# Attention and feed-forward on one core: the first batch in one pass, a later first feed-forward chunk, and another way to split float64 weights

## The chip, the cores and the metric

One Trainium2 chip, of which the program uses one core. The metric is the device time of one execution in microseconds. The engines are named as in the profile: PE (TensorE, with PEld for its weight loads), DVE (VectorE), ACT (ScalarE), POOL (GpSimd) and SP (SyncE, which issues all the transfers here).

## The reference: what is computed

Attention over 8 batches of 8 heads (576 rows, head width 64) in which, row by row, only the scores within tau of the row's maximum count; then a feed-forward with softplus on its 4608 tokens.

```python
scores = scale * np.matmul(q, k.transpose(0, 1, 3, 2))
thresh = np.max(scores, axis=-1, keepdims=True) - tau
scores = np.where(scores >= thresh, scores, -1000000000.0)
attn = np.exp(scores - np.max(scores, axis=-1, keepdims=True))
attn = attn / (np.sum(attn, axis=-1, keepdims=True) + 1e-09)
x = (attn @ v), heads side by side            # [4608, 512] float32
h = x @ w_in                                  # w_in [512, 2048], float64
g = np.maximum(h, 0.0) + np.log1p(np.exp(-np.abs(h)))
out = (g @ w_out).astype(np.float32)          # w_out [2048, 512], float64
```

The two weight matrices arrive as float64, everything else as float32.

## The kernel before

**Numbers.** Every matrix product is done on float32r words, a high and a low one: `hi_of` rounds to the high word, `lo_of` subtracts it, and products of three parts (high by high, high by low, low by high) are added in PSUM. So each weight element, too, has to become a high and a low word.

**Attention.** A *unit* is a batch and a pair of heads; a *tile* is 128 query rows of a unit. A unit has nine tiles; there are 32 pairs of batch and heads, so 288 tiles. For each unit, POOL splits k, q and v (`split_k`, `split_q`, `split_v`), PE transposes them and ACT copies them out. For each tile PE makes the scores (`scores`), DVE takes the row maximum (`row_max`, L397), ACT the exponential (`exps`, L405), DVE masks and sums (`mask`, L410), PE transposes the weights (`weights_T`, L441), ACT and DVE split them (`weights_hi`, `weights_lo`, L462 and L124), and PE multiplies by v (`values`).

**Feed-forward.** A *chunk* of tokens goes through `hidden` (PE, 16 blocks of w_in), `softplus` (ACT), `parts_of` (DVE and POOL) and `project` (PE, w_out), whose sums are collected by `project_out`. One matmul of 512 columns is a unit of work here; a chunk of 512 tokens has 384 of them (192 in `hidden`, 192 in `project`), one of 256 tokens half as much. `stream` is one long generator of these matmuls, and the main loop draws some of them at each attention tile. `target(g)` says how many shall be done by tile g: chunk n runs evenly from tile `first[n]` to `first[n + 1]`, the last two and what is left after the attention at their own pace.

**The first batch in two passes.** With `NSPLIT = 1` the first batch goes through each pair of heads twice: units of kind "one" (tiles 0, 1, 5, 6, so the first 256 rows of both heads) for four pairs, then units of kind "two" (the other five tiles) for the same four pairs. Each pass loads, splits and transposes k, and loads and splits v, again. The first two chunks then have 256 tokens, and the first of them can begin as soon as the four units "one" are done:

```python
first.append((b * 9 + (4 if b < NSPLIT and o < 256 else 9)) * NPAIR + (LAG0 if b < NSPLIT else LAG))
```

With `LAG0 = LAG = 8` that is tile 24 for the first chunk, 44 for the second, and 80, 116, 152 and so on for those of 512 tokens.

**Weights.** `to_f32` makes the words of one piece (128 rows of 512 weights); there are 32 pieces, taken from the list `WL` one every `W1` tiles. A piece is loaded (512 KB), then worked on in `first` two tiles later and in `second` one tile later. Its words of w_in are stored to `wi_d` in DRAM (two transfers of 256 KB), from which each chunk loads its blocks again (512 KB each, 16 per chunk); those of w_out stay in SBUF. Six DVE operations, two of ACT (three for w_out) and one of POOL make a piece.

**Order.** All engines take their instructions in order, and a scheduler sets each engine's order when the program is built. PSUM has two score banks (`banks`) and four others (`ps_g`). Where `row_max` and `weights_T` compare with `TG`, an early tile has its threshold made by ACT (L399) and its transposes put into `ps_g`; a later one has the threshold made by DVE (L401) and the transposes put into its own score bank.

Of the kernel before, what the change touches and what calls it, by code (L numbers as in the profile page):

```python
# [10 lines left out]
F32R = mybir.dt.float32r  # L11
U32 = mybir.dt.uint32
AF = mybir.ActivationFunctionType
ALU = mybir.AluOpType
# [7 lines left out]
W_MIN = 2.0  # L22
W_MAX = (122880.0 - 2.0 ** -7) * 2.0 ** 16
# [16 lines left out]
WS = 3  # L40
LT = 4
WB = 3
NSPLIT = 1
LAG = 8
NMM = 10.3
HD = (1, 1)
# [1 line left out]
PAIR = 2  # L48
NST = 4
GV = 1  # L50
TG = 45
W1 = 1.1
W0 = 1
SPA = 0

# [2 lines left out]
def tile_kernel(ctx: ExitStack, tc: tile.TileContext, q, k, v, tau, w_in, w_out, out):  # L58
# [8 lines left out]
    nc = tc.nc  # L67
# [7 lines left out]
    NPAIR = H // 2  # L75
# [30 lines left out]
                            op0=ALU.is_ge, op1=ALU.mult)  # L106
# [8 lines left out]
    def hi_of(eng, out_, in_):  # L115
        if eng is nc.gpsimd:
            eng.tensor_scalar(out=out_, in0=in_, scalar1=1.0, scalar2=1.0, op0=ALU.mult, op1=ALU.mult)
        elif eng is nc.scalar:
            eng.copy(out_, in_)
        else:  # L120
            eng.tensor_copy(out_, in_)  # L121

    def lo_of(eng, out_, in_, hi):
        eng.tensor_tensor(out=out_, in0=in_, in1=hi.bitcast(F32), op=ALU.subtract)  # L124
# [8 lines left out]
    def to_f32(src, want, name, then):  # L133

        keep = 1 if want else 0
        while free[0] < 3 + keep and free[0] < NFC - held[0]:
            force()
        if free[0] >= 3 + keep:
            took = 3
            fm = piece(F32, f"wa_{name}")  # L140
            f, m = fm[:, 0, :], fm[:, 1, :]
            s = piece(F32, f"wb_{name}")[:, 0, :]
            st = piece(U32, f"wc_{name}").rearrange("p a n -> p (a n)")
        else:
            took = 0
            st = fpool.tile([P, 2, DM], U32, tag="acc", name=f"wc_{name}").rearrange("p a n -> p (a n)")
            f, m, s = [fpool.tile([P, 512], F32, tag="st", bufs=NST, name=f"w{t}_{name}") for t in ("sw", "se", "st")]
        free[0] -= took + keep
        held[0] += keep
        w = piece(F32R, f"wo_{name}") if want else None  # L150

        def done():
            free[0] += took

        if src.dtype == F32:
            nc.sync.dma_start(f, src)

            def parts(h, l):
                hi_of(nc.scalar, h.bitcast(F32R), f)
                lo_of(nc.gpsimd, l, f, h.bitcast(F32R))  # L160
            defer(WD, lambda: then(parts, w, m, s, done))
            return
        nc.sync.dma_start(st, src.bitcast(U32))
        words = st.rearrange("p (n t) -> p n t", t=2)
        low, high = words[:, :, 0], words[:, :, 1]
        fu, mu, su = f.bitcast(U32), m.bitcast(U32), s.bitcast(U32)

        def first():  # L170
            nc.scalar.activation(m, high.bitcast(F32), AF.Abs, scale=2.0 ** 16)
            nc.vector.tensor_scalar(out=fu, in0=high, scalar1=23, scalar2=None, op0=ALU.logical_shift_left)
            nc.vector.scalar_tensor_tensor(out=fu, in0=low, scalar=9, in1=fu,
                                           op0=ALU.logical_shift_right, op1=ALU.bitwise_or)
            nc.scalar.activation(f, fu, AF.Copy, scale=2.0 ** -43)
            nc.vector.tensor_scalar(out=m, in0=m, scalar1=W_MIN, scalar2=W_MAX, op0=ALU.max, op1=ALU.min)
            nc.vector.tensor_scalar(out=mu, in0=mu, scalar1=3, scalar2=0xFFFFF000,
                                    op0=ALU.logical_shift_left, op1=ALU.bitwise_and)
            defer(1, second)

        def second():
            nc.vector.scalar_tensor_tensor(out=su, in0=high, scalar=0x80000000, in1=mu,
                                           op0=ALU.bitwise_and, op1=ALU.bitwise_or)
            nc.vector.tensor_scalar(out=mu, in0=su, scalar1=0xFF800000, scalar2=None, op0=ALU.bitwise_and)

            def parts(h, l):
                if w is not None:
                    hi_of(nc.scalar, h, s)
                nc.gpsimd.tensor_tensor(out=l, in0=f, in1=m, op=ALU.mult)
            then(parts, w, s, f, done)  # L190

        defer(WD, first)

    ready = set()
# [58 lines left out]
    for b in range(B):  # L253
        for kind in (("one", "two") if b < NSPLIT else ("all",)):
            for hp in range(NPAIR):
                s = Unit()
# [137 lines left out]
    def row_max(s, t):  # L394
        negm = apool.tile([P, 1], F32, tag="negm", bufs=3, name=f"negm_{s.i}_{t}")
        thr = apool.tile([P, 1], F32, tag="thr", bufs=3, name=f"thr_{s.i}_{t}")
        nc.vector.reduce_max(negm, s.sp[t][:, :, 0:HS], axis=AX.XY, negate=True)  # L397
        if 9 * NPAIR * s.b + t < TG:
            nc.scalar.activation(thr, negm, AF.Identity, bias=ntau, scale=-1.0)  # L399
        else:  # L400
            nc.vector.tensor_scalar(out=thr, in0=negm, scalar1=-1.0, scalar2=ntau, op0=ALU.mult, op1=ALU.add)  # L401
        s.m[t] = (negm, thr)
# [24 lines left out]
    def weights_T(s, t):  # L427
        half = s.half[t]
        e = e_all[:, half, :]
        other, second = mate(s, t)  # L430
        lone = other is None
        if s.b * 9 * NPAIR + t < TG:
            main = ps_g.tile([P, NC, P], F32, tag="g", name=f"tm_{s.i}_{t}")
            rest = ps_g.tile([P, NC, P], F32, tag="g", name=f"tr_{s.i}_{t}")[:, 0, :] if lone or second else None
        else:
            sp = s.sp[t]
            main = sp[:, 0, :].rearrange("p (c n) -> p c n", n=P)
            rest = sp[:, 1, 0:P]
        for c in range(NC):
            c0 = half * SR + c * P  # L440
            nc.tensor.transpose(main[:, c, :], e[:, c0:c0 + P], ident)  # L441
        if lone:
            r0 = 0 if half else SM
            nc.tensor.transpose(rest[0:SR, :], e[:, r0:r0 + SR], ident)
        elif second:
            nc.tensor.transpose(rest, e_all.rearrange("p h n -> p (h n)")[:, SM:SM + P], ident)  # L446
        s.sp[t] = (main, rest)
# [85 lines left out]
    def load_x(u, cc):  # L533
# [3 lines left out]
        while c < u.T:  # L537
            b, o = divmod(u.t0 + c, S)
            m = min(S - o, u.T - c)
            for kind in (("all",) if b >= NSPLIT else ("one", "two")[o >= 256:1 + (o + m > 256)]):  # L540
                need("x", b, cc, kind)
# [176 lines left out]
    def defer(n, f):  # L718
        if n == 0:
            f()  # L720
        else:
            later.append((now["p"] + n, f))
# [11 lines left out]

    tiles = [(s, t) for s in units for t in s.tiles]
    NS = len(tiles)
    WL = [("i", 0), ("i", 1), ("o", 0), ("i", 2), ("i", 3), ("o", 1), ("o", 2), ("o", 3)]

    chunks, first = [], []
    while sum(u.T for u in chunks) < NT:  # L740
# [4 lines left out]
        b, o = divmod(u.t0 + u.T - 1, S)  # L745
# [107 lines left out]
    done = 0.0  # L853
    for g, (cur, t) in enumerate(tiles):
# [5 lines left out]
        for step in PAT:  # L860
# [20 lines left out]
            elif step == "w":  # L881
                while prep and prep[0][0] <= g:
                    _, f, a = prep.pop(0)
# [41 lines left out]
```

## Time and profile before

| | us |
|---|---|
| three runs | 1540.53, 1544.3, 1549.28; median 1544.3 |
| the profiled execution | 1545.64 |
| its span, first to last instruction | 1543.5 |
| busy in the span: PE, DVE, ACT, POOL | 1410.7, 1073.9, 917.8, 588.1 |
| exponentials (L405), one per tile | first at 18.8, last at 1335.1 |

The exponential of a tile is the clock of this document: "tile 44 at 271.8" means that the 45th instruction of L405 began 271.8 us after the first instruction. Stretches between such times show what a tile costs in each part of the program. A busy PE is not PE at its peak: its matmuls overlap, and their ends are modelled. Durations of neighbouring instructions overlap a little as well, so sums of durations exceed busy times.

### The profile page before, as it was taken

How to read it: one execution, taken by the hardware profiler on the slowest of the kernel's cores; microseconds unless marked ns; L12 is line 12 of the kernel's file. 1: busy time of each engine (PE TensorE's matmuls, PEld its weight loads, DVE VectorE, ACT ScalarE, POOL GpSimd, SP SyncE). 2: the span in 40 equal slices, each digit the busy share in tenths (PEclk: the TensorE clock that was granted, in tenths of full speed). 3: DMA queues.
4: the chain of work that ended last, by engine and by line, in shares of the span. 5: the costliest groups of instructions: out<-in, count | busy, mean ns of one | idle time of the engine just before them, and what ended most of it. 6: DMA issues, size and time to landing. Idle time of an engine off the chain costs nothing.

```text
span 1543.5 us, 24467 instructions
## 1 busy us (share of the span) xinstructions
PE 1410.7 (91%) x8076; PEld 1202.7 (78%) x8076; DVE 1073.9 (70%) x2372; ACT 917.8 (59%) x1861; POOL 588.1 (38%) x612
## 2 busy tenths in 40 slices
PE   4555778889899999999999999999999999999998
PEld 4444767778788888888888888888888888878887
DVE  7999798778777777777777777777777777511212
ACT  5565676677576657666776576666666666511110
POOL 4554445334243334334433433344334332242321
PEclk9776899999999999999999999999999999999999
DMA  6767764544343355434443353335334532352331
GB/s 171 217 184 207 244 204 133 172 132 127 106 126 113 108 130 144 116 112 118 149 115 104 100 160 102 108 110 147 111 106 114 146 105 77 101 173 96 118 101 41
DMA packets 142030, 202.44 MB, mean 131 GB/s; under 512 B 38192, under 2 KB 97872, under 8 KB 141904
## 3 DMA queue, kind: packets, MB, share of 16 engines
q1 hardware_dynamic: 141904, 200.89, 44.6%
q8 instruction: 64, 1.05, 0.3%
q14 instruction: 62, 0.51, 0.1%
HBM read 152.44 MB, written 27.41 MB: 117 GB/s over the span
## 4 chain that ended last, share of the span: by engine, by line
PE 61%; ACT 10%; DVE 8%; issue 4%; DMA 3%; POOL 2%; SPq 1%; POOLq 0%; ACTq 0%; DVEq 0%
PE s L391 8%; PE o L636 6%; PE o L632 6%; PE o L634 6%; PE h L574 6%; PE s L441 6%; PE h L576 6%; PE h L578 6%; PE pv L485 3%; PE pv L486 3%; ACT L596 2%; DVE e_all L410 2%; ACT gH L462 2%; ACT st L596 2%; ACT L405 1%
## 5 line engine op out<-in xcount | busy, mean ns | idle before, releaser
L124 POOL TENSOR_TENSOR g<-st,g 128x512 fp32r<-128x512 f32 x144 | 193.2, 1359 | 206.3 <-DVE g L121 206.3
L410 DVE SCALAR_TENSOR_TENSOR e_all<-s,thr,e_all 128x576 f32<-128x576 f32 x288 | 234.7, 816 | 34.8 <-ACT e_all L405 29.6
L576 PE MATMUL h<-xl,wi 128*128 128x512 f32 (+1 forms) x640 | 246.4, 385 | 0.0
L574 PE MATMUL h<-xh,wi 128*128 128x512 f32 (+1 forms) x640 | 244.4, 382 | 1.1 <-DMA wi<-wi_d 0.5
L578 PE MATMUL h<-xh,wi 128*128 128x512 f32 (+1 forms) x640 | 242.8, 379 | 0.0
L397 DVE TENSOR_REDUCE negm<-s 128x1 f32<-128x576 f32 x288 | 216.9, 754 | 29.6 <-PE s L391 25.6
L636 PE MATMUL o<-wo_o,g 128*128 128x512 f32 x576 | 231.6, 402 | 4.9 <-POOL g L124 4.9
L632 PE MATMUL o<-wo_o,g 128*128 128x512 f32 x576 | 233.5, 405 | 1.7 <-ACT st L596 1.4
L634 PE MATMUL o<-wo_o,g 128*128 128x512 f32 x576 | 229.6, 399 | 0.0
L405 ACT ACTIVATE e_all<-s,negm 128x576 f32<-128x576 f32 x288 | 214.0, 743 | 7.8 <-DVE negm L397 5.9
L391 PE MATMUL s<-kT,qT 128*128 128x288 f32 x1024 | 201.1, 317 | 5.1 <-DMA qT<-qT 2.1
L124 DVE TENSOR_TENSOR gL<-s,gH 128x512 fp32r<-128x512 f32 (+1 forms) x240 | 150.2, 634 | 74.5 <-ACT gH L465 38.9
L462 ACT CAST gH<-s 128x512 fp32r<-128x512 f32 (+1 forms) x240 | 129.0, 550 | 120.5 <-PE s L446 65.6
L391 PEld LDWEIGHTS s<-kT,qT 128*128 128x128 f32 x1024 | 153.6, 196 | 23.8 <-DVE gH L124 14.7
L121 DVE CAST g<-st 128x512 fp32r<-128x512 f32 x144 | 67.0, 502 | 149.5 <-ACT st L596 148.9
L485 PE MATMUL pv<-gH,vt 128*128 128x320 f32 (+1 forms) x512 | 148.4, 310 | 1.4 <-ACT gH L462 1.4
L596 ACT ACTIVATE st<-h 128x512 f32<-128x512 f32 x144 | 78.5, 596 | 117.8 <-PE h L578 117.1
L486 PE MATMUL pv<-gL,vt 128*128 128x320 f32 (+1 forms) x512 | 146.1, 305 | 0.0
L574 PEld LDWEIGHTS h<-xh,wi 128*128 128x128 f32 x640 | 123.9, 194 | 22.5 <-ACT gH L462 0.7
L441 PE MATMUL s<-identr,e_all 128*128 128x128 f32 x864 | 135.2, 279 | 6.9 <-DVE e_all L410 5.9
L578 PEld LDWEIGHTS h<-xh,wi 128*128 128x128 f32 x640 | 123.2, 193 | 19.4
L576 PEld LDWEIGHTS h<-xl,wi 128*128 128x128 f32 x640 | 123.8, 193 | 18.6
(107 smaller groups left out, 2558.9 us busy)
## 6 DMA issues: line engine op xcount, KB each, us to landing
wi<-wi_d SPq DMA_DIRECT2D x160, 512.0 KB
qT<-qT SPq DMA_DIRECT2D x112, 128.0 KB
kn<-in_k_dram SPq DMA_DIRECT2D x36, 256.0 KB
qn<-in_q_dram SPq DMA_DIRECT2D x36, 256.0 KB
vn<-in_v_dram SPq DMA_DIRECT2D x36, 256.0 KB
wc_i<-in_moe_w_in_dram SPq DMA_DIRECT2D x16, 512.0 KB
wc_o<-in_moe_w_out_dram SPq DMA_DIRECT2D x16, 512.0 KB
R<-r_d SPq DMA_DIRECT2D x56, 144.0 KB
```

The source lines that it names most:

```text
L124: eng.tensor_tensor(out=out_, in0=in_, in1=hi.bitcast(F32), op=ALU.subtract)
L391: nc.tensor.matmul(sp[:, hf, 0:HS], lhs, s.kT[j][:, k0 + hf * HS:k0 + (hf + 1) * HS], start=(m == 0), stop=(m == len(parts) - 1))
L397: nc.vector.reduce_max(negm, s.sp[t][:, :, 0:HS], axis=AX.XY, negate=True)
L405: nc.scalar.activation(e_all[:, s.half[t], :].rearrange("p (h n) -> p h n", h=2), s.sp[t][:, :, 0:HS], AF.Exp, bias=s.m[t][0], scale=1.0)
L410: nc.vector.scalar_tensor_tensor(out=e2, in0=s.sp[t][:, :, 0:HS], scalar=s.m.pop(t)[1], in1=e2, op0=ALU.is_ge, op1=ALU.mult, accum_out=s.s ...
L441: nc.tensor.transpose(main[:, c, :], e[:, c0:c0 + P], ident)
L574: nc.tensor.matmul(h, wi[:, 0, cc, :], u.h[cc], start=(cc == 0), stop=False)
L576: nc.tensor.matmul(h, wi[:, 0, cc, :], u.l[cc], start=False, stop=False)
L578: nc.tensor.matmul(h, wi[:, 1, cc, :], u.h[cc], start=False, stop=(cc == NCC - 1))
L632: nc.tensor.matmul(o, gh[:, sl], wo[fc][:, 0, :], start=(i == 0), stop=False)
L634: nc.tensor.matmul(o, gh[:, sl], wo[fc][:, 1, :], start=False, stop=False)
L636: nc.tensor.matmul(o, gl[:, sl], wo[fc][:, 0, :], start=False, stop=(i == QF - 1))
```

## The change

Three things change.

1. `NSPLIT = 0`: the first batch runs as units of kind "all", nine tiles each, like the other batches: 32 units instead of 36, nine chunks of 512 tokens instead of two of 256 and eight of 512. The first chunk has `first = 9 * 4 + 8 = 44`. So it runs from tile 44 to tile 80, 384 matmuls over 36 tiles; before, 192 ran from tile 24 to 44 and 192 from 44 to 80. From tile 80 on the chunks stand as before.
2. `to_f32` for float64. Before: the low part was made from bits on DVE (L172, L173), scaled on ACT (L175), multiplied on POOL (L189) by a power of two cut out on DVE (L184). Now: ACT takes the absolute value (as before), POOL clamps it (min and max, on DVE before, L176), one tile later DVE shifts it (L176 in the new numbering, L177 before), takes over the sign (L177, before L182) and puts in the top bits of the low word (L179). One tile after that ACT rounds the high word, for w_in too, and POOL subtracts it. A piece now has three operations on DVE (six before), two on POOL (one before) and two on ACT (before two for w_in and three for w_out), and takes one tile longer.
3. The numbers: `WL` takes all of w_in first, `W1` goes from 1.1 to 1.25 tiles per piece (the last of 32 pieces is taken at tile 39, before at 35). `TG` is 36 and now counts tiles exactly: ACT's threshold and `ps_g` hold for the first 36 tiles; before, the condition left out the unit, and they held for all 72 tiles of the first two batches.

```diff
-NSPLIT = 1
+NSPLIT = 0
...
-TG = 45
-W1 = 1.1
+TG = 36
+W1 = 1.25
...
         def first():
             nc.scalar.activation(m, high.bitcast(F32), AF.Abs, scale=2.0 ** 16)
-            nc.vector.tensor_scalar(out=fu, in0=high, scalar1=23, scalar2=None, op0=ALU.logical_shift_left)
-            nc.vector.scalar_tensor_tensor(out=fu, in0=low, scalar=9, in1=fu,
-                                           op0=ALU.logical_shift_right, op1=ALU.bitwise_or)
-            nc.scalar.activation(f, fu, AF.Copy, scale=2.0 ** -43)
-            nc.vector.tensor_scalar(out=m, in0=m, scalar1=W_MIN, scalar2=W_MAX, op0=ALU.max, op1=ALU.min)
-            nc.vector.tensor_scalar(out=mu, in0=mu, scalar1=3, scalar2=0xFFFFF000,
-                                    op0=ALU.logical_shift_left, op1=ALU.bitwise_and)
+            nc.gpsimd.tensor_scalar(out=m, in0=m, scalar1=W_MAX, scalar2=W_MIN, op0=ALU.min, op1=ALU.max)
             defer(1, second)
 
         def second():
+            nc.vector.tensor_scalar(out=mu, in0=mu, scalar1=3, scalar2=None, op0=ALU.logical_shift_left)
             nc.vector.scalar_tensor_tensor(out=su, in0=high, scalar=0x80000000, in1=mu,
                                            op0=ALU.bitwise_and, op1=ALU.bitwise_or)
-            nc.vector.tensor_scalar(out=mu, in0=su, scalar1=0xFF800000, scalar2=None, op0=ALU.bitwise_and)
+            nc.vector.scalar_tensor_tensor(out=su, in0=low, scalar=29, in1=su,
+                                           op0=ALU.logical_shift_right, op1=ALU.bitwise_or)
 
             def parts(h, l):
-                if w is not None:
-                    hi_of(nc.scalar, h, s)
-                nc.gpsimd.tensor_tensor(out=l, in0=f, in1=m, op=ALU.mult)
-            then(parts, w, s, f, done)
+                h = h.bitcast(F32R)
+                hi_of(nc.scalar, h, s)
+                lo_of(nc.gpsimd, l.bitcast(F32R), s, h)
+            defer(1, lambda: then(parts, w, f, m, done))
...
-        if 9 * NPAIR * s.b + t < TG:
+        if 9 * NPAIR * s.b + 9 * s.hp + t < TG:
             nc.scalar.activation(thr, negm, AF.Identity, bias=ntau, scale=-1.0)
...
-        if s.b * 9 * NPAIR + t < TG:
+        if 9 * NPAIR * s.b + 9 * s.hp + t < TG:
             main = ps_g.tile([P, NC, P], F32, tag="g", name=f"tm_{s.i}_{t}")
...
-    WL = [("i", 0), ("i", 1), ("o", 0), ("i", 2), ("i", 3), ("o", 1), ("o", 2), ("o", 3)]
+    WL = [("i", 0), ("i", 1), ("i", 2), ("i", 3), ("o", 0), ("o", 1), ("o", 2), ("o", 3)]
```

**What moves on DVE.** Some rows of DVE before, from the mask of tile 14 of the program to that of tile 15; in the names, `wa`, `wb` and `wc` are a weight piece's words and its load, `o2` is piece 2 of w_out, `negm` the row maximum, `e_all` the masked exponentials, `gL` the low words of the attention weights.

```order
L410 SCALAR_TENSOR_TENSOR e_all_140,sums_3_837<-s_0_141,thr_3_5_981,e_all_140 128x576
L172 TENSOR_SCALAR wa_o2_957<-wc_o2_959 128x512
L176 TENSOR_SCALAR wa_o2_957<-wa_o2_957 128x512
L173 SCALAR_TENSOR_TENSOR wa_o2_957<-wc_o2_959,wa_o2_957 128x512
L177 TENSOR_SCALAR wa_o2_957<-wa_o2_957 128x512
L397 TENSOR_REDUCE negm_3_6_1041<-s_1_142 128x1
L182 SCALAR_TENSOR_TENSOR wb_o2_958<-wc_o2_959,wa_o2_957 128x512
L124 TENSOR_TENSOR gL_3_1_1039<-tm_3_5_1033,gH_3_1_1038 128x4x128
L184 TENSOR_SCALAR wa_o2_957<-wb_o2_958 128x512
L410 SCALAR_TENSOR_TENSOR e_all_140,sums_3_837<-s_1_142,thr_3_6_1042,e_all_140 128x576
```

And of DVE now, from the mask of tile 14 to that of tile 15 (all lines after the changed part are four lower, so L393 is the row maximum and L406 the mask).

```order
L406 SCALAR_TENSOR_TENSOR e_all_136,sums_1_556<-s_0_137,thr_1_5_814,e_all_136 128x576
L176 TENSOR_SCALAR wa_i2_1_790<-wa_i2_1_790 128x512
L393 TENSOR_REDUCE negm_1_6_868<-s_1_138 128x1
L177 SCALAR_TENSOR_TENSOR wb_i2_1_791<-wc_i2_1_792,wa_i2_1_790 128x512
L124 TENSOR_TENSOR gL_1_2_809<-tm_1_5_862,gH_1_2_808 128x4x128
L179 SCALAR_TENSOR_TENSOR wb_i2_1_791<-wc_i2_1_792,wb_i2_1_791 128x512
L406 SCALAR_TENSOR_TENSOR e_all_136,sums_1_556<-s_1_138,thr_1_6_869,e_all_136 128x576
```

Between two masks, six instructions of a weight piece became three; the first of them now takes its input from POOL.

**What moves on PE.** Before, the first rows of the feed-forward, at tile 24 (`h` is the hidden bank, `xh` and `xl` the words of the tokens, `tm` a tile's transposed weights).

```order
L391 MATMUL s_1_142<-kT_5_1_1364,qT0_5_1_1368 128x288 x2
L391 MATMUL s_1_142<-kT_5_1_1364,qT1_5_1_1369 128x288 x2
L441 MATMUL tm_5_7_1610<-identr_81,e_all_140 128x128 x4
L574 MATMUL h_0_0_1646<-xh_0_0_1624,wi_0_0_1640 128x256
L576 MATMUL h_0_0_1646<-xl_0_0_1625,wi_0_0_1640 128x256
L578 MATMUL h_0_0_1646<-xh_0_0_1624,wi_0_0_1640 128x256
```

And now, at tile 44.

```order
L437 MATMUL s_0_137<-identr_81,e_all_136 128x128 x4
L442 MATMUL s_0_137<-identr_81,e_all_136 128x128
L481 MATMUL pv_4_2_2217<-gH_4_2_2082,vt_4_1_1736 128x320
L570 MATMUL h_0_0_2276<-xh_0_0_2252,wi_0_0_2270 128x512
L572 MATMUL h_0_0_2276<-xl_0_0_2253,wi_0_0_2270 128x512
L574 MATMUL h_0_0_2276<-xh_0_0_2252,wi_0_0_2270 128x512
```

No matmul of the feed-forward stands on PE ahead of tile 44 any more, and the transposes beside it go into the score bank `s` and not into `tm`.

**What moves on POOL.** POOL now, around tiles 30 to 32 (`wo` are the words of w_out, `xp` a unit's output, `R` its row scales, which come by a transfer).

```order
L172 TENSOR_SCALAR wa_o6_1550<-wa_o6_1550 128x512
L124 TENSOR_TENSOR wo_o5_1511<-wb_o5_1509,wo_o5_1511 128x512
L518 TENSOR_TENSOR xp_2_1159<-xp_2_1159,R_2_1561 128x576
L172 TENSOR_SCALAR wa_o7_1602<-wa_o7_1602 128x512
L124 TENSOR_TENSOR wo_o6_1553<-wb_o6_1551,wo_o6_1553 128x512
```

The clamp L172, for which DVE's first instruction of a piece waits, is queued behind such a scaling of a unit's output.

More of the change, by code (lines that the diff above doesn't have):

```diff
@@ L165, in to_f32 @@
         low, high = words[:, :, 0], words[:, :, 1]
-        fu, mu, su = f.bitcast(U32), m.bitcast(U32), s.bitcast(U32)
+        mu, su = m.bitcast(U32), s.bitcast(U32)
         def first():
             nc.scalar.activation(m, high.bitcast(F32), AF.Abs, scale=2.0 ** 16)
-            nc.vector.tensor_scalar(out=fu, in0=high, scalar1=23, scalar2=None, op0=ALU.logical_shift_left)
-            nc.vector.scalar_tensor_tensor(out=fu, in0=low, scalar=9, in1=fu,
-                                           op0=ALU.logical_shift_right, op1=ALU.bitwise_or)
-            nc.scalar.activation(f, fu, AF.Copy, scale=2.0 ** -43)
-            nc.vector.tensor_scalar(out=m, in0=m, scalar1=W_MIN, scalar2=W_MAX, op0=ALU.max, op1=ALU.min)
-            nc.vector.tensor_scalar(out=mu, in0=mu, scalar1=3, scalar2=0xFFFFF000,
-                                    op0=ALU.logical_shift_left, op1=ALU.bitwise_and)
+            nc.gpsimd.tensor_scalar(out=m, in0=m, scalar1=W_MAX, scalar2=W_MIN, op0=ALU.min, op1=ALU.max)
             defer(1, second)
         def second():
+            nc.vector.tensor_scalar(out=mu, in0=mu, scalar1=3, scalar2=None, op0=ALU.logical_shift_left)
             nc.vector.scalar_tensor_tensor(out=su, in0=high, scalar=0x80000000, in1=mu,
                                            op0=ALU.bitwise_and, op1=ALU.bitwise_or)
-            nc.vector.tensor_scalar(out=mu, in0=su, scalar1=0xFF800000, scalar2=None, op0=ALU.bitwise_and)
+            nc.vector.scalar_tensor_tensor(out=su, in0=low, scalar=29, in1=su,
+                                           op0=ALU.logical_shift_right, op1=ALU.bitwise_or)
             def parts(h, l):
-                if w is not None:
-                    hi_of(nc.scalar, h, s)
-                nc.gpsimd.tensor_tensor(out=l, in0=f, in1=m, op=ALU.mult)
-            then(parts, w, s, f, done)
+                h = h.bitcast(F32R)
+                hi_of(nc.scalar, h, s)
+                lo_of(nc.gpsimd, l.bitcast(F32R), s, h)
+            defer(1, lambda: then(parts, w, f, m, done))
         defer(WD, first)
```

## The prediction

> **What bounds the kernel now.** I read the page first, for where PE stands idle.
>
> ```profile
> span 1543.5 us, 24467 instructions
> PE   4555778889899999999999999999999999999998
> PEclk9776899999999999999999999999999999999999
> ```
>
> Each digit is a slice of 38.6 us. From slice 10 on (some 390 us) PE is busy nine tenths and more: that part is bound by PE. The first seven slices are not, and the clock granted to PE sinks there with its work. Everything that the change touches lies in them, or moves work out of them. Then the exponentials of L405, by windows that end just after the start of tile 24, 44, 80, 116 and 152.
>
> ```profile
> L405 ACT ACTIVATE e_all<-s,negm x25: 716/727/752, 18.8 to 149.6; 128x576 f32<-128x576 f32 x25
> L405 ACT ACTIVATE e_all<-s,negm x45: 716/731/767, 18.8 to 271.8; 128x576 f32<-128x576 f32 x45
> L405 ACT ACTIVATE e_all<-s,negm x81: 716/734/772, 18.8 to 414.4; 128x576 f32<-128x576 f32 x81
> L405 ACT ACTIVATE e_all<-s,negm x117: 716/741/779, 18.8 to 572.1; 128x576 f32<-128x576 f32 x117
> L405 ACT ACTIVATE e_all<-s,negm x153: 716/742/779, 18.8 to 732.8; 128x576 f32<-128x576 f32 x153
> ```
>
> The last time in each row is the start of that tile. Tiles 24 to 44 take 122.2 us, 6.1 each, with 9.6 feed-forward matmuls per tile; tiles 116 to 152 take 160.7 us, 4.5 each, with 10.7 of them. So the early tiles are slow for another reason. Windows between these times show it.
>
> ```profile
> core 0: us, PE busy (x) PEld busy (x) DVE busy (x) ACT busy (x) POOL busy (x), PEclk, DMA share, GB/s
> 0.00:18.80 18.80, 5.22 (x22) 3.87 (x22) 9.88 (x19) 7.13 (x15) 8.47 (x15) 1.00 0.57 164
> 18.80:53.95 35.15, 20.74 (x124) 19.00 (x124) 31.25 (x66) 23.26 (x57) 19.17 (x25) 0.82 0.66 189
> 53.95:149.62 95.67, 50.19 (x264) 45.18 (x264) 92.43 (x184) 59.93 (x145) 48.61 (x56) 0.70 0.68 198
> 149.62:271.84 122.22, 95.88 (x600) 85.77 (x601) 103.90 (x210) 86.36 (x184) 60.78 (x63) 0.90 0.62 197
> 271.84:414.42 142.58, 126.14 (x854) 111.54 (x853) 106.93 (x236) 95.45 (x219) 50.32 (x56) 0.96 0.47 134
> 414.42:572.12 157.70, 155.68 (x917) 132.10 (x916) 119.71 (x275) 106.62 (x209) 61.45 (x64) 1.00 0.42 120
> 572.12:732.81 160.69, 158.65 (x934) 135.12 (x933) 120.78 (x276) 106.72 (x209) 61.38 (x64) 1.00 0.44 122
> ```
>
> Tiles 8 to 24 (53.95 to 149.62) are DVE's: 92.4 of 95.7 us, 97%. Tiles 24 to 44 are still mostly DVE's (85%). Tiles 80 on are PE's (99%). So the stretch up to tile 44 is priced by DVE, the stretch from 44 to 80 by PE once it has full chunks, and what comes after tile 80 has the same work in both kernels.
>
> **Term 1: DVE up to tile 44.** DVE's busy time to 271.84 is 9.88 + 31.25 + 92.43 + 103.90 = 237.5 us. Of that, the weight operations and the first chunk's have these shares; one row for each line, in the order L172, L173, L176, L177, L182, L184, L121 (high words of softplus), L649 (sums of the projection).
>
> ```profile
> 0.00:271.84 271.84, 18.73 (x32) 0.82 0.64 194
> 0.00:271.84 271.84, 26.59 (x32) 0.82 0.64 194
> 0.00:271.84 271.84, 17.39 (x32) 0.82 0.64 194
> 0.00:271.84 271.84, 18.67 (x32) 0.82 0.64 194
> 0.00:271.84 271.84, 24.10 (x32) 0.82 0.64 194
> 0.00:271.84 271.84, 19.01 (x32) 0.82 0.64 194
> 0.00:271.84 271.84, 4.89 (x8) 0.82 0.64 194
> 0.00:271.84 271.84, 3.38 (x5) 0.82 0.64 194
> ```
>
> Of the six, L177 (the shift) and L182 (the sign) stay, and the new L179 has the form of L173: strided words of the load and a tile in SBUF. L172, the clamp L176 and L184 go: 18.73 + 17.39 + 19.01 = 55.1 us. The feed-forward's 8.3 us move behind tile 44, together 63.4. What is left is 237.5 - 63.4 = 174 us. That is the low end: durations of neighbours overlap, and what is removed may have been long only because it waited.
>
> ```profile
> L172 DVE TENSOR_SCALAR wa_i<-wc_i x16: 415/423/1370, 10.7 to 146.9; 128x512 uint32<-128x512 uint32 x16
> L173 DVE SCALAR_TENSOR_TENSOR wa_i<-wc_i,wa_i x16: 677/684/1643, 11.2 to 147.6; 128x512 uint32<-128x512 uint32 x16
> ```
>
> These rows give minimum, median and maximum: half of L172's take 0.42 us. At that price the 96 operations are 41 us, and 237.5 - 41 - 8 = 188 us is the high end. I take 180, nearer to the low end, since the windows show what these operations did cost in place. Eight thresholds that go from ACT to DVE at tiles 36 to 43 are under 2 us of it.
>
> How much of the time DVE will be busy is the second unknown. The start to the first exponential (18.8 us, 9.9 of them busy) stays as it is: it waits for the first loads. For the remaining 170 us of work the rows give 97% (tiles 8 to 24, where weight work filled every hole) and 85% (tiles 24 to 44). With fewer weight operations there is less to fill holes, so I take 91%: 187 us, and tile 44 at 206 us. The ends are 164/0.97 + 19 = 188 and 179/0.85 + 19 = 229.
>
> Do other engines allow that? ACT's busy time to tile 44 is 7.1 + 23.3 + 59.9 + 86.4 = 176.7 us and loses more than it gains (one operation in each w_out piece, the softplus of the first chunk, the copies of four units): under 170 of 206. PE loses the first chunk's matmuls. POOL's is 8.5 + 19.2 + 48.6 + 60.8 = 137.0 us; these are its rows up to there.
>
> ```profile
> L124 POOL TENSOR_TENSOR vt<-vn,vt 128x320 fp32r<-128x320 f32 x20 | 18.1, 907 | 1.3
> L124 POOL TENSOR_TENSOR k<-kn,k 128x576 fp32r<-128x576 f32 x9 | 15.1, 1682 | 0.5
> L117 POOL TENSOR_SCALAR vt<-vn 128x320 fp32r<-128x320 f32 x20 | 10.6, 534 | 44.0 <-PE pv L487 33.2 <-DMA vn<-in_v_dram 6.8 <-DMA wc_i<-in_moe_w_in_dram 3.8
> L117 POOL TENSOR_SCALAR k<-kn 128x576 fp32r<-128x576 f32 x9 | 7.7, 853 | 3.2 <-PE tr L328 3.0
> ```
>
> The clamp has the form of L117 on k with 512 elements for 576: 0.85 x 512/576 = 0.76 us, 32 times, 24 us more. The subtraction replaces a multiplication of the same form. Four units fewer take away 4 x (0.85 + 1.68 + 2 x 0.53 + 2 x 0.91) = 22 us. POOL stays near 137 us of 206 (67%): hidden, if its results come in time.
>
> Transfers: 194 GB/s for 271.8 us are 52.7 MB. The first chunk's 16 blocks of 512 KB (8.4 MB) and k and v of four units (2.4 MB) leave it: some 42 MB in 206 us, 204 GB/s, about what the rows above held anyway.
>
> **Term 2: tiles 44 to 80.** Here stand 384 matmuls now, 192 before. That is the load of tiles 80 to 116 and 116 to 152, which took 157.7 and 160.7 us at 99% of PE. I take 160.5. The threshold on DVE and the transposes in the score bank are those stretches' too, so they are in that price. The entry costs something on top. Before, the first matmuls of the feed-forward (256 columns) ran at half the pace of later ones:
>
> ```profile
> 153.46 0.41 PE L578 MATMUL h<-xh,wi 128*128 128x256 f32 x1
> 153.67 0.41 PE L574 MATMUL h<-xh,wi 128*128 128x256 f32 x1
> ...
> 161.62 0.28 PE L574 MATMUL h<-xh,wi 128*128 128x256 f32 x1
> 161.73 0.28 PE L576 MATMUL h<-xl,wi 128*128 128x256 f32 x1
> ```
>
> Starts are 0.21 us apart, then 0.11; this lasted for some 4 us, so 2 us are lost. And the first chunk needs the last unit's output eight tiles after that unit ends, through a scaling that waits for a transfer. In the stretch from tile 44 to 80 before, such waits were
>
> ```profile
> POOL xp L522 <- DMA R<-r_d: 22.0, 3, 10.1
> ```
>
> (total, times, longest). Between nothing and 10 us I take 1.5, since eight tiles of 4.2 us are 34 us. Entry 3.5 us, term 2 is 164 us, with 158 and 171 as ends. Tile 80 comes at 206 + 164 = 370 instead of 414.4.
>
> **Sum.** 414.4 - 370 = 44.4 us less, from the profiled execution's 1545.6: 1501.2. The median of the runs, 1544.3, is 1.3 us lower, so 1500. The units of 256 columns that vanish I price at nothing in PE's part: their starts, 0.11 us for 256 columns, are in proportion to their size.
>
> **Rivals.**
>
> *The hand-off stalls DVE (slower).* DVE's first instruction of a piece now waits for POOL's clamp, and with it every mask and row maximum queued behind. POOL in turn may stand at a scaling that waits for `R` ahead of the clamp. The nearest row is the opposite hand-off, POOL waiting for DVE in the same work:
>
> ```profile
> POOL wo_o L189 <- DVE wa_o L184: 13.9, 8, 3.7
> ```
>
> 1.7 us each time. If each of 32 pieces costs DVE that, 55 us eat the 44 and the kernel ends at 1555. It decides from 44.4/32 = 1.4 us a piece. Against it: the shift stands a tile after the clamp in the program. 10%.
>
> *POOL holds DVE back.* L173's maximum, 1643 ns against a minimum of 677, is an instruction with two SBUF inputs that lost 0.97 us; its sum, 26.59 us for 32, is 0.15 us above the median each. After the change two of the three operations have that form, and POOL has one more in each piece. If the loss for each of the 96 grows from 0.15 to 0.30 us, 14 us more: 1515. The Trainium skill ("SBUF — State Buffer", section "Who interferes with whom") says that DVE instructions with two SBUF inputs or in a two-port mode and POOL's share one pair of ports, and that the loser waits for the whole of the other's instruction. The maximum above agrees, the medians show that it seldom happens. 11%.
>
> *Transfers bind.* All of w_in comes first now. Up to tile 20 I count 16 pieces of 1 MB in and out and 5 MB for attention, 22 MB. In the 100 us that my DVE price gives these tiles, this is 220 GB/s. Tiles 8 to 24 held 198; the best 12 us had more:
>
> ```profile
> 156.00:168.00 12.00, 10.85 (x82) 10.28 (x81) 10.08 (x23) 9.02 (x19) 2.73 (x3) 0.94 0.82 282
> ```
>
> If 198 is all that lasts, or if late loads stop ACT, tile 44 comes 11 to 25 us later: about 1520. 14%.
>
> *DVE stays full.* With DVE busy 97% of the time and 158 us for tiles 44 to 80, tile 80 comes at 348: 1478. 13%.
>
> **How the numbers follow.** My forecast, 1500 (1486 to 1514), has 52%; the four rivals 10, 11, 14 and 13%. The predicted time is 1500. The range from 1478 to 1530 holds all but the hand-off's 10% and the far ends of the others. This measurement can tell about 0.5% from no change, 8 us: faster below 1536.6, slower above 1552. Faster: all but the hand-off, 90%. The hand-off's share I split at its price: 4% within 0.5%, 6% slower.
>
> **What would show it.** The 45th exponential near 206 us and the 81st near 370, with DVE at 85% or more and about 180 us busy before the 45th. The 81st to the 117th in 158 to 161 us. DVE's waits for POOL's clamp under 20 us in all, and ACT's waits for `wc` loads no longer than before. Wrong would be: an early pace of over 5 us a tile with DVE idle (hand-off or transfers, told apart by who ended its waits), or over 171 us for tiles 44 to 80.

## The result, and the profile after

The changed kernel took 1526.5 us, the median of four runs (1526.1 to 1528.9), beside 1542.4 us of the kernel before on the same chip. The ratio is 0.9892, 95% interval [0.9858, 0.9927]: 1.1% faster. The forecast was 1500 from 1544.3: a gain of 44 us, of which 16 came. The profiled execution took 1528.9 us and its span 1527.1.

The head of the page of the changed kernel: the span, and the busy share of PE and its granted clock in 40 slices of 38.2 us.

```profile
span 1527.1 us, 23624 instructions
PE   4556569999999999999999999999999999999998
PEclk9766679999999999999999999999999999999999
```

PE is now full from slice 7 on (its start is at 229 us); before it was slice 10 (from 347 us; the 390 of the prediction is nearly this slice's end). The clock returns with it; in the slices ahead of it its digits are 6 and 7. Then the exponentials by windows that end just after the start of tile 44, 80 and 116; the last time in a row is that start.

```profile
L401 ACT ACTIVATE e_all<-s,negm x45: 719/732/752, 18.0 to 237.9; 128x576 f32<-128x576 f32 x45
L401 ACT ACTIVATE e_all<-s,negm x81: 719/740/779, 18.0 to 395.9; 128x576 f32<-128x576 f32 x81
L401 ACT ACTIVATE e_all<-s,negm x117: 719/742/781, 18.0 to 556.2; 128x576 f32<-128x576 f32 x117
```

| start of | before | forecast | after |
|---|---|---|---|
| tile 44 | 271.8 | 206 | 237.9 |
| tile 80 | 414.4 | 370 | 395.9 |
| tile 116 | 572.1 | 528 to 531 | 556.2 |

Tile 44 came 31.9 us later than forecast, tiles 44 to 80 took 158.0 us where I had 164 (6.0 less), tiles 80 to 116 took 160.3 where they had taken 157.7 (2.6 more), and the rest of the execution was 0.8 us shorter. Together 27.7 us, which is 1528.9 less 1501.2. So the miss is in the stretch up to tile 44. Windows of the changed kernel, cut at tile 0, 8, 24, 36 and 44:

```profile
core 0: us, PE busy (x) PEld busy (x) DVE busy (x) ACT busy (x) POOL busy (x), PEclk, DMA share, GB/s
0.00:18.00 18.00, 5.49 (x27) 4.48 (x27) 4.82 (x11) 6.59 (x15) 6.77 (x15) 1.00 0.57 148
18.00:49.70 31.70, 19.16 (x117) 18.27 (x117) 26.74 (x54) 21.63 (x52) 14.21 (x16) 0.89 0.71 202
49.70:129.80 80.10, 46.15 (x234) 41.75 (x233) 73.75 (x139) 48.97 (x117) 41.66 (x46) 0.69 0.78 220
129.80:196.20 66.40, 38.14 (x193) 34.85 (x191) 57.68 (x102) 40.38 (x91) 34.45 (x38) 0.68 0.52 158
196.20:237.90 41.70, 28.02 (x129) 24.13 (x129) 28.63 (x65) 21.84 (x49) 19.76 (x22) 0.67 0.30 81
237.90:395.90 158.00, 156.07 (x917) 132.32 (x917) 119.64 (x275) 106.45 (x210) 61.29 (x64) 1.00 0.43 121
```

DVE is busy 92% of tiles 8 to 24 (97% before), 87% of tiles 24 to 36, and only 69% of tiles 36 to 44, which take 5.2 us each. No other engine is near full there. In all DVE is busy 191.6 of the 237.9 us: 11.6 more than the 180 that I took, and idle 46 instead of 26.

Two groups of DVE's waits up to 237.9 in the changed kernel (us in total, times, longest) name a new releaser:

```profile
DVE wa_o L176 <- POOL wa_o L172: 7.6, 6, 2.3
DVE wa_i L176 <- POOL wa_i L172: 7.5, 8, 2.8
```

15.1 us of the 46 are waits for POOL's clamp. And the instruction that waits has become longer. Its group in the changed kernel (minimum, median, maximum in ns), for the pieces of w_in and of w_out, and the sum over all 32 pieces:

```profile
L176 DVE TENSOR_SCALAR wa_i<-wa_i x16: 366/426/1521, 14.4 to 118.1; 128x512 uint32<-128x512 uint32 x16
L176 DVE TENSOR_SCALAR wa_o<-wa_o x13: 416/1342/1511, 127.8 to 220.5; 128x512 uint32<-128x512 uint32 x13
```

```profile
0.00:237.90 237.90, 28.30 (x32) 0.73 0.60 170
```

The shift had cost 18.67 us before, the price that I took over; now it is 28.30. Why, two pieces of the changed kernel's timeline show, of POOL and of DVE (start, duration, idle time ahead and its releaser):

```profile
156.93 0.61 POOL L172 TENSOR_SCALAR wa_o<-wa_o 128x512 f32<-128x512 f32 x1 [1.56 <-ACT wa_o L171]
157.55 1.26 POOL L124 TENSOR_TENSOR xl<-xst,xh 128x512 fp32r<-128x512 f32 x1
```

```profile
157.58 1.51 DVE L176 TENSOR_SCALAR wa_o<-wa_o 128x512 uint32<-128x512 uint32 x1 [2.28 <-POOL wa_o L172]
159.12 0.76 DVE L393 TENSOR_REDUCE negm<-s 128x1 f32<-128x576 f32 x1
```

DVE has stood 2.28 us for the clamp; POOL ends it and at once begins its next instruction, a subtraction with two inputs of 1.26 us. The shift starts 0.03 us after that and takes 1.51 us: 1.23 until POOL's instruction ends, and 0.28 more. So where POOL has its next instruction at hand, the hand-off itself puts the shift right behind that instruction's start. The row maximum of the next tile then stands behind the shift. The Trainium skill ("SBUF — State Buffer", section "Who interferes with whom") says that DVE's `tensor_scalar`, which the shift is, can run in a two-port mode and then needs the ports shared with POOL, that whoever issues first holds them for the whole instruction, and that "Issue order, not op shape, decides who blocks." These two rows agree, and so do two rows in which the shift came first, by 0.07 us: it took 0.41 us, and POOL's instruction 1.49.

```profile
118.06 0.41 DVE L176 TENSOR_SCALAR wa_i<-wa_i 128x512 uint32<-128x512 uint32 x1
118.13 1.49 POOL L124 TENSOR_TENSOR wa_i<-wb_i,wa_i 128x512 fp32r<-128x512 f32 x1 [0.21 <-ACT wa_i L119]
```

In the changed kernel's timeline 13 of the 32 shifts take over 1 us (5 of 16 for w_in, 8 of 13 for w_out), and each of the 13 began while a two-input instruction of POOL had already begun. Nine of them had waited for the clamp. The other five shifts that waited found POOL with nothing to start, and took 0.43 us.

### The profile page after: what moved, and what is told of

The parts are those of the page before. It is cut to its first block, busy times and chain, and to the rows that moved or that the text cites. A ratio compares the mean times of both kernels' runs of the same rounds, so it can differ in the third digit from the quotient of the medians.

```text
span 1527.1 us, 23624 instructions
## 1 busy us (share of the span) xinstructions
PE 1408.3 (92%) x7840; PEld 1196.1 (78%) x7840; DVE 1039.6 (68%) x2304; ACT 890.9 (58%) x1775; POOL 578.1 (38%) x596
## 4 chain that ended last, share of the span: by engine, by line
PE 66%; ACT 12%; DVE 10%; issue 7%; POOL 3%; DMA 1%; SPq 1%; ACTq 0%; POOLq 0%; DVEq 0%
PE s L387 9%; PE s L437 7%; PE o L632 7%; PE o L628 7%; PE o L630 7%; PE h L570 6%; PE h L572 6%; PE h L574 6%; PE pv L481 4%; PE pv L482 4%; ACT gH L458 2%; ACT L592 2%; DVE e_all L406 2%; ACT st L592 2%; ACT e_all L401 2%
## 5 line engine op out<-in xcount | busy, mean ns | idle before, releaser
L406 DVE SCALAR_TENSOR_TENSOR e_all<-s,thr,e_all 128x576 f32<-128x576 f32 x288 | 234.6, 815 | 26.3 <-ACT e_all L401 22.7
L393 DVE TENSOR_REDUCE negm<-s 128x1 f32<-128x576 f32 x288 | 217.1, 754 | 32.5 <-PE s L387 28.3
L458 ACT CAST gH<-s 128x512 fp32r<-128x512 f32 (+1 forms) x280 | 150.5, 551 | 142.9 <-PE s L442 75.4
L572 PE MATMUL h<-xl,wi 128*128 128x512 f32 x576 | 233.3, 405 | 0.0
L124 DVE TENSOR_TENSOR gL<-s,gH 128x512 fp32r<-128x512 f32 (+1 forms) x280 | 175.2, 634 | 82.8 <-ACT gH L461 44.3
L570 PE MATMUL h<-xh,wi 128*128 128x512 f32 x576 | 229.5, 398 | 0.0
L574 PE MATMUL h<-xh,wi 128*128 128x512 f32 x576 | 229.4, 398 | 0.0
L437 PE MATMUL s<-identr,e_all 128*128 128x128 f32 x1008 | 159.6, 281 | 6.3 <-DVE e_all L406 5.2
L481 PE MATMUL pv<-gH,vt 128*128 128x320 f32 (+1 forms) x512 | 154.0, 320 | 2.5 <-ACT gH L458 2.5
L482 PE MATMUL pv<-gL,vt 128*128 128x320 f32 (+1 forms) x512 | 151.0, 314 | 0.3 <-DVE gL L124 0.3
L437 PEld LDWEIGHTS s<-identr,e_all 128*128 128x128 f32 x1008 | 116.2, 142 | 31.9 <-DVE e_all L406 28.2
L632 PEld LDWEIGHTS o<-wo_o,g 128*128 128x128 f32 x576 | 108.4, 188 | 30.3 <-POOL g L124 11.8
L570 PEld LDWEIGHTS h<-xh,wi 128*128 128x128 f32 x576 | 108.6, 189 | 23.2
```

Of the source, the lines that this page charges most:

```text
L406: nc.vector.scalar_tensor_tensor(out=e2, in0=s.sp[t][:, :, 0:HS], scalar=s.m.pop(t)[1], in1=e2, op0=ALU.is_ge, op1=ALU.mult, accum_out=s.s ...
L570: nc.tensor.matmul(h, wi[:, 0, cc, :], u.h[cc], start=(cc == 0), stop=False)
L572: nc.tensor.matmul(h, wi[:, 0, cc, :], u.l[cc], start=False, stop=False)
L574: nc.tensor.matmul(h, wi[:, 1, cc, :], u.h[cc], start=False, stop=(cc == NCC - 1))
L632: nc.tensor.matmul(o, gl[:, sl], wo[fc][:, 0, :], start=False, stop=(i == QF - 1))
```

## The experiments

The measure is the start of tile 44, T44, beside the ratio to the kernel before (0.9892 for the changed kernel). In each row shown, the window runs from 0 to T44, with the columns of the windows above. Each ratio is to runs of the kernel before beside it, on the same chip. T44 is read from one profiled execution of each kernel: the changed kernel and the one with `TG = 44`, whose edit bears on tiles 36 to 43 alone, differ by 1.7 us at tile 8 and by 0.6 us at tile 36, so differences of some 2 us say nothing. What follows T44 takes 1290 to 1295 us in the one-pass kernels with the new split, so a gain at T44 arrives at the end but for a few us. The two kernels themselves:

```profile
0.00:271.84 271.84, 172.04 (x1010) 153.82 (x1011) 237.47 (x477) 176.69 (x396) 137.02 (x158) 0.82 0.64 194
```

```profile
0.00:237.90 237.90, 136.96 (x694) 123.48 (x695) 191.62 (x368) 139.41 (x319) 116.85 (x134) 0.73 0.60 170
```

**One pass alone.** The kernel before, with the first batch in one pass; `TG`, `W1` and the order of the pieces stay.

```
-NSPLIT = 1
+NSPLIT = 0
```

> The kernel before with NSPLIT = 0 alone: one pass for the first batch, first chunk of 512 tokens from tile 44, old six-operation weight split, old W1, WL and TG. Theory (DVE prices the tiles up to 44): DVE keeps 124 us of weight operations instead of the 77 of the changed kernel, so tile 44 comes some 40 us later than its 238, at 270 to 285 us, and the kernel ends slower than before, 1550 to 1570. Rival (the pace there is set by the tile's chain at PE's low clock, whatever DVE carries): tile 44 at 240 to 250, the kernel at 1525 to 1540.

1547.3 us, ratio 1.0027 [1.0013, 1.0041]: no gain. T44 lies in the rival's range and not in the theory's; the kernel's time lies in neither. The window of one pass alone:

```profile
0.00:249.80 249.80, 129.04 (x686) 117.97 (x687) 220.47 (x456) 151.24 (x344) 97.66 (x102) 0.75 0.56 162
```

T44 comes 22 us earlier, but tiles 44 to 80 then take 161.4 us instead of 142.6, since the first chunk's matmuls stand there, and 19 of the 22 us are given back. DVE is still 88% busy: the six weight operations cost 117 us of its 220.5.

**The new split alone.** The kernel before with the new `to_f32`, two passes.

```
-            nc.scalar.activation(f, fu, AF.Copy, scale=2.0 ** -43)
-            nc.vector.tensor_scalar(out=m, in0=m, scalar1=W_MIN, scalar2=W_MAX, op0=ALU.max, op1=ALU.min)
+            nc.gpsimd.tensor_scalar(out=m, in0=m, scalar1=W_MAX, scalar2=W_MIN, op0=ALU.min, op1=ALU.max)
...
```

> The kernel before with the new three-operation weight split alone (two passes, chunk of 256 from tile 24, W1, WL and TG as before). Theory: DVE loses 40 to 55 us of work in the first 272, part of it eaten by its waits for the clamp on POOL; tile 44 at 240 to 250, tile 80 some 143 us later, the kernel at 1512 to 1522, so faster than the whole change: what moving the chunk to tile 44 costs (16 us from tile 44 to 80) isn't spent. Rival: the one pass is what saves, by four units less, and this alone gives under 8 us: 1535 or more.

1538.7 us, ratio 0.9965 [0.9951, 0.9978]: a third of a per cent, as the rival had it. The window and DVE's waits for the clamp in it:

```profile
0.00:269.70 269.70, 171.96 (x1010) 153.12 (x1011) 202.46 (x381) 167.47 (x379) 153.95 (x190) 0.83 0.66 196
```

```profile
DVE wa_o L176 <- POOL wa_o L172: 12.0, 7, 3.8
DVE wa_i L176 <- POOL wa_i L172: 11.3, 7, 5.0
DVE wse_o L176 <- POOL wse_o L172: 3.7, 2, 2.0
```

DVE loses 35 us of work and T44 moves by 2: with two passes the cheaper split buys nearly nothing. 27 us of waits for the clamp have come in, with POOL at 154 us instead of 137. The gain is lost behind tile 24: that tile starts at 137.9 instead of 149.6, but the tiles from there to T44 then take 131.8 us instead of 122.2, with DVE busy 72% of them, in these two windows:

```profile
137.90:230.40 92.50, 63.65 (x387) 56.83 (x386) 63.66 (x116) 58.73 (x124) 50.77 (x60) 0.83 0.70 223
230.40:269.70 39.30, 33.25 (x224) 29.50 (x223) 30.75 (x62) 25.90 (x59) 22.12 (x26) 1.00 0.49 146
```

**The new split alone, without the clamp.** The last, less the clamp (so weights outside its bounds are not limited).

```
-            nc.gpsimd.tensor_scalar(out=m, in0=m, scalar1=W_MAX, scalar2=W_MIN, op0=ALU.min, op1=ALU.max)
```

> The kernel of conv_only (two passes, new weight split) without the clamp. There DVE waited 27 us for it before tile 44, with POOL's four extra units ahead of it. Theory (the hand-off ate the gain there): tile 44 at 235 to 248 instead of 269.7, the kernel 1506 to 1520, so that one pass buys nothing by itself. Rival (two passes cost by their own work on POOL and PE): tile 44 at 255 or later, the kernel 1525 or more.

1532.0 us, ratio 0.9917 [0.9896, 0.9938]: the rival's side again.

```profile
0.00:263.80 263.80, 172.92 (x1010) 155.20 (x1011) 199.08 (x381) 165.74 (x377) 135.26 (x158) 0.82 0.66 200
```

T44 moves by 6 us more and DVE is idle 65 us. So the clamp's waits are not what holds the kernel with two passes. Tile 24 starts at 135.3, and the tiles from there to T44 still take 128.5 us, more than the 122.2 before. The first chunk stands among them, but that it sets their pace is not shown, nor which of the waits there decides.

**Thresholds back.** The changed kernel, with the thresholds of tiles 36 to 43 on ACT and their transposes in a bank of their own, as before.

```
-TG = 36
+TG = 44
```

> The changed kernel with TG = 44: tiles 36 to 43, too, have their threshold on ACT and their transposes in the other PSUM banks, so that a score bank is free after the mask. Theory: the waits of the scores for the low words (8.3 us of PE in that stretch) go, those eight tiles take 32 to 36 us instead of 41.7, the kernel 1516 to 1521. Rival (PE's low clock or other waits set the pace there): 41 us as now, within 3 us of 1526.

1522.9 us, ratio 0.9862 [0.9841, 0.9882], 2 us over the theory's range, with the eight tiles inside theirs. T44 is 228.5, 9.4 us earlier. First PE's waits in tiles 36 to 44 of the changed kernel, of which this one has none, then this kernel's window of these tiles:

```profile
PE s L387 <- DVE gL L124: 8.3, 3, 4.0
PE s L387 <- DVE gH L124: 2.4, 1, 2.4
```

```profile
195.60:228.50 32.90, 18.27 (x118) 16.97 (x119) 27.38 (x58) 22.89 (x56) 18.64 (x21) 0.89 0.36 99
```

Until tile 36 both are alike (195.6 and 196.2). Then 4.1 us a tile instead of 5.2, for 1.3 us less of DVE's work. In the changed kernel the next tile's scores wait until DVE has read the transposes out of the score bank. The edit undoes the threshold on DVE as well; that the bank is the larger part is read from these waits and from DVE's 1.3 us. Of the 9.4 us, tiles 44 to 80 take 2.9 back (160.9 us instead of 158.0; the clock is 0.86 in their first 11.5 us, and was 1.00 there in the changed kernel).

**The clamp on DVE.** The changed kernel.

```
-            nc.gpsimd.tensor_scalar(out=m, in0=m, scalar1=W_MAX, scalar2=W_MIN, op0=ALU.min, op1=ALU.max)
+            nc.vector.tensor_scalar(out=m, in0=m, scalar1=W_MAX, scalar2=W_MIN, op0=ALU.min, op1=ALU.max)
```

> The changed kernel with the clamp on DVE instead of POOL: 32 operations of 0.42 us and more come to DVE (13 to 17 us), its 15.1 us of waits for POOL go, and the shift after it falls from 28.3 to 15 to 19 us. Theory (the hand-off and the port cost more than the operation): tile 44 at 222 to 232 instead of 238, the kernel 1511 to 1520. Rival (DVE's waits only move elsewhere): tile 44 at 238 to 250, the kernel 1526 to 1538.

1525.0 us, ratio 0.9871 [0.985, 0.9892]; T44 is 231.2. The sums of its clamp (first row) and of its shift over 32 pieces, and the shift of the w_out pieces:

```profile
0.00:231.20 231.20, 20.48 (x32) 0.76 0.61 175
0.00:231.20 231.20, 15.79 (x32) 0.76 0.61 175
```

```profile
L176 DVE TENSOR_SCALAR wa_o<-wa_o x13: 407/420/874, 131.7 to 219.9; 128x512 uint32<-128x512 uint32 x13
```

The shift's median falls from 1.34 to 0.42 us and its sum by 12.5 us. With the 15.1 us of waits that is 27.6 us of hand-off against 20.5 us of added work: 7.1 us, and T44 moved by 6.7. On DVE the clamp costs no more than on POOL. T44 is in the theory's range; the kernel is 5 us above its own. The clamp cost 20.5 us where 13 to 17 were expected.

**No clamp.** The changed kernel, the clamp left out.

```
-            nc.gpsimd.tensor_scalar(out=m, in0=m, scalar1=W_MAX, scalar2=W_MIN, op0=ALU.min, op1=ALU.max)
```

> The changed kernel without the clamp (the operation is left out): DVE's shift then waits for ACT alone, and POOL has one operation less in each piece. Theory (the hand-off to POOL and the blocked shift cost 15.1 us of waits and 9 to 12 us of longer shifts): tile 44 at 211 to 218 us instead of 238, the kernel 1500 to 1508. Rival (PE's low clock and the tile's chain set the pace, so DVE's waits move elsewhere): tile 44 at 230 or later, the kernel 1518 or more.

1514.5 us, ratio 0.9813 [0.9773, 0.9852].

```profile
0.00:223.60 223.60, 129.71 (x694) 117.96 (x695) 187.49 (x368) 138.63 (x318) 100.97 (x102) 0.78 0.63 181
```

T44 comes 14.3 us earlier, later than the 211 to 218 of the theory: of the 27.6 us of the hand-off about half is worth time. The 15.1 us of waits for the clamp go, but the shift now waits 7.7 us for ACT's absolute value. The shift's sum falls by 9.0 us, to 19.3, but DVE's busy sum by 4.1 us only, as the two operations behind the shift lengthen by 4.4 us.

**No clamp, thresholds back.** Both edits at once.

```
-TG = 36
+TG = 44
...
-            nc.gpsimd.tensor_scalar(out=m, in0=m, scalar1=W_MAX, scalar2=W_MIN, op0=ALU.min, op1=ALU.max)
```

> The changed kernel without the clamp and with TG = 44, the two suspected losses together. Theory: they add up, tile 44 at 202 to 209, the kernel 1492 to 1500, where the prediction had it. Rival (a common limit under both): no more than the larger of the two alone, tile 44 at 215 or later.

1511.6 us, ratio 0.9787 [0.9749, 0.9825].

```profile
0.00:218.60 218.60, 130.70 (x682) 119.92 (x683) 184.38 (x360) 140.26 (x326) 98.17 (x102) 0.75 0.64 185
```

T44 is 19.3 us earlier than in the changed kernel, less than 14.3 and 9.4 together: the two overlap, which is nearer to the rival than to the 202 to 209 of the theory. 12.6 us beyond the forecast remain. DVE is here busy 184.4 us, 4.4 more than I took, and idle 34.2, 8.2 more.

**The shift a tile later.** The changed kernel.

```
-            defer(1, second)
+            defer(2, second)
```

> The changed kernel with the DVE part of a piece two tiles after the clamp instead of one. Theory (DVE comes to the shift before POOL has got to the clamp): DVE's waits for the clamp fall from 15.1 us to under 5, tile 44 at 225 to 231, the kernel 1514 to 1520. Rival (the scheduler puts the shift right behind the clamp again, or what is saved is lost to port conflicts): within 3 us of 1526.

1522.8 us, ratio 0.9862 [0.9819, 0.9906]; T44 is 231.6. Its groups of waits for the clamp sum to 8.1 us, down from 15.1; this is the largest:

```profile
DVE wa_i L176 <- POOL wa_i L172: 4.6, 3, 2.7
```

So the tile that stands between clamp and shift in the program is not enough time for all pieces. The waits did not fall under 5 us, as the theory had it, and T44 and the kernel's time lie just above its ranges.

**The same, thresholds back.** `defer(2, second)` and `TG = 44`.

> The changed kernel with the DVE part two tiles after the clamp and TG = 44, nothing left out. Theory: the two gains (6.3 and 9.4 us at tile 44) add at least in part, tile 44 at 222 to 228, the kernel 1512 to 1519, the quickest complete one. Rival: one hides the other, 1520 or more.

1520.5 us, ratio 0.9843 [0.982, 0.9866]; T44 is 225.4. This is the quickest version that leaves nothing out: better than the kernel before, and some 0.5% better than the changed kernel, though the two intervals still touch. T44 is in the theory's range, but the kernel's time in the rival's.

**Less work on DVE.** The kernel without clamp and with the thresholds back, less the third operation (so the last three bits of each word are missing).

```
-            nc.vector.scalar_tensor_tensor(out=su, in0=low, scalar=29, in1=su,
-                                           op0=ALU.logical_shift_right, op1=ALU.bitwise_or)
```

> The kernel of no_clamp_tg44 (tile 44 at 218.6 us) without DVE's third operation of a piece (the low bits of the high word are left out): some 23 us less on DVE before tile 44, nothing else touched. Theory (DVE prices these tiles): tile 44 falls by nearly that, to 196 to 201. Rival (the tile's chain through PE and ACT sets the pace): it falls by less than half, 208 or later.

1497.5 us, ratio 0.9696 [0.9667, 0.9724].

```profile
0.00:204.90 204.90, 117.86 (x684) 108.15 (x685) 163.86 (x328) 139.79 (x327) 95.00 (x102) 0.83 0.69 198
```

20.5 us less of DVE's work brought T44 forward by 13.7, two thirds: between the theory's 196 to 201 and the rival's 208. DVE is the first limit of this stretch, but it isn't alone. One pass alone and `TG = 44` give nearly the same price: both have one pass and the old thresholds in these tiles, and 29.4 us less work on DVE bring T44 from 249.8 to 228.5, 21.3 us (`W1` and the order of the pieces differ as well).

**Less work on PE.** The same base; of each nine matmuls with `v` in the first batch, two are left, so its attention output is incomplete.

```
-        for c in range(NC):
+        short = s.b == 0
+        for c in range(0 if short else NC):
...
+        if short:
+            nc.tensor.matmul(o[:, 0:n], vt[:, 0, :], l[:, NC - 1, 0:n], start=True, stop=False)
```

> The kernel of no_clamp_tg44 with two of nine matmuls in each product with v of the first batch (the other seven are left out): some 30 us less on PE before tile 44, nothing less on DVE. Theory (DVE): tile 44 within 5 us of 218.6. Rival (PE's work at its low clock stands in the chain): tile 44 at 210 or earlier.

1516.0 us, ratio 0.9816 [0.9783, 0.9849]; T44 is 223.0, 4.4 us later. The same stretch (47 to 125 us) of this kernel and, below, of its base:

```profile
47.00:125.00 78.00, 45.95 (x198) 40.36 (x199) 74.12 (x145) 51.89 (x121) 35.68 (x33) 0.52 0.82 230
```

```profile
47.00:125.00 78.00, 49.20 (x250) 45.37 (x249) 73.79 (x141) 50.71 (x119) 33.12 (x32) 0.70 0.80 229
```

A fifth of the matmuls is gone and PE's busy time falls by 7% only, while the clock sinks from 0.70 to 0.52. So the amount of PE's work isn't what holds these tiles. Up to T44 PE's busy time fell by 8.9 us and not by the 30 that were meant, so the run doesn't exclude that PE's steps, at its low clock, lengthen the way of each tile.

**PE kept busy.** The changed kernel with 16 more matmuls in each of tiles 4 to 39, into columns of the score bank that nothing reads.

```
+                if 4 <= g < 40:
+                    for _ in range(16):
+                        nc.tensor.matmul(banks[g % SB][:, 1, 288:512], identr, tiles[g + 2][0].kT[0][:, 0:224],
+                                         start=True, stop=True)
```

> The changed kernel with 16 extra matmuls of 224 columns per tile from tile 4 to 39, into PSUM columns that nobody reads, which keep PE busy. If PE's low clock (0.67 to 0.69 there) sets the pace, the clock goes to 0.9 or more and tile 44 comes at 228 or earlier, the kernel at 1517 or less. Theory (DVE prices these tiles): tile 44 within 5 us of 238, 1522 to 1532.

1594.4 us, ratio 1.0326 [1.0287, 1.0365]; T44 is 302.9.

```profile
50.00:150.00 100.00, 56.91 (x348) 54.58 (x348) 72.01 (x121) 48.53 (x105) 46.18 (x51) 0.72 0.74 217
```

In this window the clock was 0.72 only (the changed kernel had 0.69 in tiles 8 to 24), and the added matmuls stand ahead of the transposes that DVE waits for. So the run doesn't tell what the early tiles would take at the full clock. That stays open.

## Why the prediction was right in direction and wrong in size

*Direction and place: right.* The gain is in the stretch up to tile 44, and DVE's work there is its first limit: less of it brought time, at two thirds of its price. Neither half of the change does it alone (1.0027 and 0.9965; both 0.9892): with one pass the first chunk leaves the stretch, and there the cheaper split shortens it; with two passes it hardly did. The new pace `W1` and the order of the pieces were not run by themselves.

*Term 2: right.* 158.0 us against 164, on my low end. The entry of 3.5 us didn't come: the clock was 1.00 over the stretch from tile 44 on, and there is no slow start to see in its 156.1 busy us.

*Term 1: the step that failed,* 237.9 instead of 206, and 9 us over its high end of 229. It joined two numbers, and both came out at their bad ends or beyond.

The busy time, 180, became 191.6. I moved the shift over at its old price, 18.67, though its input now comes from another engine; it cost 28.30, which in its own row is 9.6 of the 11.6 us. Besides, I let the start keep its 9.9 us of work; it had 4.8, and the rest came behind it. So 186.8 us of work stood behind the start where I had 170, and at my 91% that alone is some 18 us of the miss.

The busy share after the start, taken as 91%, was 85% ((191.6 - 4.8) of (237.9 - 18.0)), the other 14 us. Two things pressed it down: the waits for the clamp (15.1 us), and the loop over the score bank in tiles 36 to 43. Of that edit I had priced only DVE's work on the thresholds, "under 2 us", which is about what it was; the bank I put at nothing in these tiles. Undone together they were worth 9.4 us, with only 1.3 us of DVE's work in it. The transposes I had called part of the later stretches' price, where PE is the bound and the loop is hidden; in tiles 36 to 43 nothing hides it.

With both taken away T44 is 218.6, and the busy share behind the start is 90% (180.2 us of 200.4), nearly what I took. So the remaining 12.6 us are mostly work: 10 us more behind the start than my 170, over half of which I had left in the start. Which rows hold the rest is open. Open too is what beside DVE holds these tiles, since less work on DVE paid only two thirds: a way through PE at its low clock (0.67 to 0.69) is the rival that no run here settles.

*The hand-off rival* was real but smaller than priced: 0.47 us of wait a piece, not 1.7, and on top 0.30 us a piece of a longer shift, which is the ports' rival in another instruction than the one I had named. I had set the two against each other with a chance each; they came together, because nine of the 14 waits for the clamp ended in such a collision. POOL was busy 116.9 us up to tile 44, less than the 137 that I took; its room did not keep the waits away. Under my bound "waits under 20 us" the waits looked harmless.

*Transfers* show no limit: tiles 8 to 24 drew 220 GB/s, above the 198 that I had feared as a ceiling, and ACT's waits for the loads of weight pieces were 8.4 us in the changed kernel, by these rows, and 8.9 before.

```profile
ACT wa_i L171 <- DMA wc_i<-in_moe_w_in_dram: 4.9, 3, 2.0
ACT wa_o L171 <- DMA wc_o<-in_moe_w_out_dram: 3.5, 3, 2.0
```

*DVE stays full* failed for the reason of term 1. Its 348 us doesn't come out of its own terms either: 170 us of work at 97% are 175 us, and with the start and 158 us for tiles 44 to 80 that is 352.

## What to carry to other kernels

Work that is moved from a full engine to one with room isn't free when the full engine must take the result back: price the wait of the first instruction behind the hand-off, and that instruction again at a collision with whatever the other engine starts next (here 27.6 us for 32 pieces, more than the 20.5 us that the step costs on the full engine). A buffer that is shared between two steps lengthens the loop through it; take its price from a stretch where the same engine is the bound, not from one in which another engine hides it. And on an engine that is busy nine tenths of a stretch, work taken away is not worth its whole duration: here it was two thirds.

## What the runs showed that I had not expected

A shift of 128x512 words that takes 0.42 us took 1.07 to 1.52 us in 13 of 32 pieces, each time behind a two-input instruction of POOL that had just begun. With the same clamp on DVE only one of the 32 took over 1 us, and the sum was 15.8 us instead of 28.3.

Taking matmuls away from an early stretch that PE doesn't bound lowered the granted clock from 0.70 to 0.52 (47 to 125 us) and gave no time; adding 16 a tile to the changed kernel left it at 0.72 (50 to 150 us).
